# Layer norm sums moved from VectorE to ScalarE in a delta-rule attention kernel with two gated MLPs

## The chip, the cores and the metric

The kernel runs on one core of one Trainium2 chip. A core has TensorE (PE in the profile, with PEld for its weight loads), VectorE (DVE), ScalarE (ACT), GpSimd (POOL) and SyncE (SP), which here only issues DMAs. Each engine takes its instructions strictly in the order of its own list; between engines semaphores tell when something may start. The metric is the device time of one execution in microseconds (us), lower is better; a time of a kernel is the median of several runs.

## The reference

Three blocks follow one another, for batch 4, 8 heads, 768 positions, head size 48, so that the model width is 384:

```
state = 0                                   # delta-rule attention, per head
for t in range(S):
    y[t]  = q[t] @ state
    state = state + beta[t] * outer(kn[t], v[t] - kn[t] @ state)      # kn = k / |k|

gate = sigmoid(causal_conv5(y));  x = (gate * (y @ w_val)) @ w_out    # first MLP

h = gelu_tanh(x @ w_in)                     # second MLP; d_ff = 1024
u, v = h[:, :512], h[:, 512:]
v_n  = (v - mean(v)) / sqrt(var(v) + 1e-6) * g_ln                     # over the 512 features
v_s  = w_sg @ v_n + b_sg                    # mixes the 768 positions of a batch
out  = x + (u * v_s) @ w_out2
```

## The kernel before

**Attention.** The sequences are cut into chunks of 64 positions: 4 batches of 12 chunks, 48 steps (`seq(n)` and `attend(n)`), which follow one another, since each needs the state of the one before. Ahead of them the triangular systems of two chunks at a time are prepared (`norm`, `keys`, `gram`, `base`, `merge`); `base` solves for 8 chunks at once on VectorE, on tiles named X and tmp. Nearly every fp32 result is split into a high and a low fp16 half: ScalarE copies to the high half, then VectorE (or GpSimd) subtracts to get the low one, and TensorE multiplies halves in three passes (`mm3`). A step of the recurrence so goes back and forth between TensorE, ScalarE and VectorE (tiles rh, wh, mh, ys, qh, ps_q, ps_y, ps_state).

**MLPs.** Positions go in tiles of 256 (`TT`), 3 to a batch. `front` loads the attention's output and makes the gate, `value` the gated values (gvh), `hidden` the half v of the second MLP with its layer norm, `gates` the half u, `mix` the mixing of positions by w_sg (PE tile wg,vnh), `final` the output. `mix` of a batch needs the normed tiles (vnh) of all six position blocks of 128 in that batch, so all three calls of `hidden`.

**The layer norm in `hidden`.** There are 12 calls of `hidden`, each with two blocks (`NS` = 2) of 128 positions on the partitions and 512 features along the row, 24 blocks in all. For each block, ScalarE writes v = gelu(ps); VectorE takes BN_STATS of v (tile st) and BN_AGGR of st to mean and variance (tile mv). For both blocks together, VectorE then scales the variance and negates the mean (two small TENSOR_SCALAR, tile va), GpSimd raises the variance to the power -1/2 (rd) and multiplies the mean by it (mb). ScalarE norms in place, v = v * rd + mb, and copies to the high half of vnh, and GpSimd subtracts for the low half.

**Order.** A planner in the kernel (`Program`) records every operation with its tiles, takes the order of each engine from a table (`ORDER`, one list of numbers for each of the five engines), and runs through it with a cost for each operation (`cost`). Where it expects TensorE to wait over 0.3 us, it may put in a filler: a matmul that adds to an unused half of the bank ps_state (`filler`, operand minus). The fillers are in the program for good. All instructions are issued through one helper line, L108, so groups are told apart by tiles.

Of the kernel before, what the change touches and what calls it, by code (L numbers as in the profile page):

```python
# [39 lines left out]
class Program:  # L40
# [41 lines left out]
    def add(self, engine, method, call, kw):  # L82
# [3 lines left out]
        for k in ("out",) + self.READS:  # L86
            m = self.memory.get(kw[k].tensor.name) if isinstance(kw.get(k), bass.AP) else None
            if m:
                touched.append((m, k == "out", self.region(kw[k], m)))
# [123 lines left out]
class Pool:  # L213
# [5 lines left out]
    def tile(self, shape, dtype, name, tag=None, **kw):  # L219
# [233 lines left out]
def cost(op):  # L453
# [13 lines left out]
    if engine == "scalar":  # L467
        if apart:
            t = 0.00225 * n - (0.113 if psum else 0.07)
            return t, t + 0.26, False  # L470
# [925 lines left out]
```

## Time and profile before

| what | value |
|---|---|
| median of 3 runs | 647.62 us |
| lowest and highest of them | 646.28 and 649.8 us |
| the profiled execution, whole | 646.62 us |
| its span, first to last instruction | 644.7 us |
| granted TensorE clock, mean | 0.991 |

The profile is of one execution. Its own time is 1.92 us over its span, and 1.0 us under the median. A row of the profile gives an engine, an operation, the tiles it writes and reads, and its durations; idle time of an engine is listed by what ended it.

### The profile page before, as it was taken

Reading aid. Unit: us, or ns where it says so; the run is one execution under the profiler, and the core shown is the slowest. Engines: PE = TensorE matmul, PEld = TensorE weight load, DVE = VectorE, ACT = ScalarE, POOL = GpSimd, SP = SyncE. Lnnn points to the kernel's source line nnn. Section 1 sums busy time; section 2 is a strip of 40 time slices with the busy share of each in tenths; the row PEclk is TensorE's granted clock in tenths of the full one; section 3 lists DMA queues with packets and bytes.
Section 4 is the critical chain, followed back from the end, with each engine's and each line's share of the span. In section 5 each row is a group of like instructions: output and inputs, shape, how many; then the busy total and the mean of one; then the engine's idle time right before and its main releaser. Section 6 shows DMA issues by size and latency. Waiting matters only on the chain. (4 is left out here: it accounts for less than half of the span.)

```text
span 644.7 us, 23559 instructions
## 1 busy us (share of the span) xinstructions
PE 575.0 (89%) x9821; PEld 473.8 (73%) x9821; DVE 503.1 (78%) x1341; ACT 398.2 (62%) x932; POOL 179.6 (28%) x204
## 2 busy tenths in 40 slices
PE   0678879779979989799999999889999999999997
PEld 0555446668767767688888689778978897877886
DVE  7898998979889998988999879899887854562222
ACT  7886697756876767775466785344948544524221
POOL 7404041126423625366001650001605010303000
PEclk9999998989999998999999999999999999999999
DMA  7664367877579776687678778788687763211121
GB/s 223 160 202 132 126 189 235 186 156 165 107 182 175 134 122 146 128 195 132 163 143 179 145 123 170 121 140 152 120 155 141 107 142 102 63 50 34 58 82 50
DMA packets 288826, 89.22 MB, mean 138 GB/s; under 512 B 250704, under 2 KB 276944, under 8 KB 288720
## 3 DMA queue, kind: packets, MB, share of 16 engines
q1 hardware_dynamic: 288720, 87.72, 63.0%
q8 instruction: 77, 1.26, 0.9%
q14 instruction: 29, 0.24, 0.1%
HBM read 51.81 MB, written 23.33 MB: 117 GB/s over the span
## 5 line engine op out<-in xcount | busy, mean ns | idle before, releaser
L108 PE MATMUL ps_mlp<-wg,vnh 128*128 128x256 f16 x864 | 112.4, 272 | 1.4 <-DVE ps_mlp L108 1.4
L108 PEld LDWEIGHTS <-vnh 128*128 128x128 f16 x864 | 80.5, 97 | 12.0 <-issue 2.1
L108 PEld LDWEIGHTS <-kj 112*128 112x128 f16 (+1 forms) x1632 | 69.2, 97 | 21.4 <-issue 12.7
L108 PEld LDWEIGHTS <-kc 64*64 64x64 f16 x1920 | 42.1, 113 | 47.5 <-DVE kc L108 20.8
L108 PE MATMUL ps_mlp<-gvh,wi 128*128 128x256 f16 x432 | 58.0, 272 | 1.2 <-ACT v L108 0.8
L108 PE MATMUL ps_mlp<-gth,w 128*128 128x256 f16 x432 | 58.8, 272 | 0.0
L108 DVE TENSOR_TENSOR tmp<-X 128x84 f32<-128x84 f32 (+12 forms) x156 | 56.1, 360 | 1.4
L108 DVE TENSOR_TENSOR X<-X,tmp 128x84 f32<-128x84 f32 (+12 forms) x156 | 54.5, 349 | 1.5
L108 PE MATMUL ps_mlp<-wi,gvh 128*128 128x512 f16 x216 | 54.7, 379 | 0.6 <-ACT gvh L108 0.4
L108 DVE SCALAR_TENSOR_TENSOR ps_mlp<-ps_mlp,gl,bs 128x256 f32<-128x256 f32 x48 | 23.4, 488 | 34.3 <-PE ps_mlp L108 33.9
L108 DVE SCALAR_TENSOR_TENSOR a<-x,cw,a 128x256 f32<-128x256 f32 x108 | 48.8, 486 | 1.6 <-ACT a L108 1.3
L108 PE MATMUL ps_mlp<-xh,wv 128*128 128x256 f16 x324 | 45.7, 272 | 2.2 <-ACT xh L108 2.1
L108 PE MATMUL ps_mlp<-gvh,wo 128*128 128x256 f16 x324 | 47.1, 272 | 0.1
L108 PEld LDWEIGHTS <-m1p 128*128 128x128 f16 x1152 | 39.5, 96 | 9.9 <-issue 5.7
L108 PE MATMUL pk<-i,kc 64*64 64x64 f16 x704 | 22.5, 200 | 27.2 <-DVE kc L108 20.0
L108 PEld LDWEIGHTS <-wi 128*128 128x128 f16 x432 | 40.3, 97 | 6.4 <-issue 1.3
L108 PEld LDWEIGHTS <-w 128*128 128x128 f16 x432 | 40.8, 98 | 5.0
L108 PE MATMUL ps_y<-qh,kj 112*128 112x64 f16 x576 | 32.8, 193 | 4.2 <-ACT ys L108 4.1
L108 POOL TENSOR_TENSOR X<-X,bm 128x1024 f32<-128x1024 f32 x5 | 11.8, 2353 | 87.4 <-DVE X L108 72.0
L108 PEld LDWEIGHTS <-ws 128*128 128x128 f16 (+1 forms) x828 | 32.2, 98 | 4.9 <-issue 3.2
L108 PEld LDWEIGHTS <-wo 128*128 128x128 f16 x342 | 31.8, 97 | 5.5 <-issue 0.9
L108 POOL TENSOR_TENSOR vnh<-v,vnh 128x512 f16<-128x512 f32 x24 | 27.9, 1170 | 25.6 <-ACT vnh L108 25.5
(165 smaller groups left out, 1451.5 us busy)
## 6 DMA issues: line engine op xcount, KB each, us to landing
keys_d<-kc SPq DMA_DIRECT2D x22, 512.0 KB, 4.1
kj<-keys_d SPq DMA_DIRECT2D x44, 256.0 KB, 5.0
wg<-wgd SPq DMA_DIRECT2D x12, 768.0 KB, 4.8
ws<-wh SPq DMA_DIRECT2D x66, 96.0 KB, 3.6
qf<-in_qt SPq DMA_DIRECT2D x24, 224.0 KB, 3.5
kf<-in_kn SPq DMA_DIRECT2D x12, 384.0 KB, 4.7
vf<-in_vn SPq DMA_DIRECT2D x24, 192.0 KB, 3.4
xd<-ys SPq DMA_DIRECT2D x48, 96.0 KB, 3.0
```

What stands on the lines that cost most here:

```text
L108: op.call()
```

## The change

The statistics of the layer norm are no longer taken by VectorE. The Gelu pass on ScalarE writes, beside v, the sum of its 512 results to a tile `sums` (accum_out). GpSimd multiplies that sum by -1/512, which gives the negated mean (va). A new ScalarE pass then takes the square of v plus that negated mean, again with an accumulator, which gives the sum of the squared deviations; its 512 squares are written into the high half of vnh, which the later copy overwrites. GpSimd scales this sum to the variance. BN_STATS, BN_AGGR and the two TENSOR_SCALAR go; 24 Square passes on ScalarE and 36 small operations on GpSimd (24 of 128x1, 12 of 128x2) come. The planner learns that accum_out is written, and adds 0.093 to ScalarE's cost where there is one. All five lists of the order are made anew; the numbers in them say nothing to a reader, and one line stands for them.

```diff
-        for k in ("out",) + self.READS:
+        for k in ("out", "accum_out") + self.READS:
...
-                touched.append((m, k == "out", self.region(kw[k], m)))
+                touched.append((m, k in ("out", "accum_out"), self.region(kw[k], m)))
...
-        "3 14 18 6 13 16 0 12 15 5 22 19 24 11 20 25:2 10 47 17 4 7 1 8 35 2 21 23 32 38 9 37 36 34 33 28 30 29 31 "
+        "6 0 3 20:2 1 14 16 13 24 8 12 15 11 25:2 22 10 18 35 32 38 9 2 7 47 17 37 19 36 34 33 5 4 23 28 30 29 31 "
...
     if engine == "scalar":
+        more = 0.093 * ("accum_out" in op.kw)
...
-        return t, t + 0.1, False
+        return t + more, t + more + 0.1, False
...
-        mv = mp.tile([P, NS, 2], F32, name="mv", tag="mv", bufs=2)
+        sums = mp.tile([P, 2, NS], F32, name="sums", tag="mv", bufs=2)
+        va = mp.tile([P, 2, NS], F32, name="va", tag="va", bufs=2)
...
-            nc.scalar.activation(out=v, in_=ps, func=AF.Gelu_apprx_tanh, scale=1.0 / (SGV * SWI))
-            st = mp.tile([P, 6], F32, name="st", tag="st", bufs=2)
-            nc.vector.bn_stats(out=st, in_=v)
-            nc.vector.bn_aggr(out=mv[:, i], in_=st)
+            nc.scalar.activation(out=v, in_=ps, func=AF.Gelu_apprx_tanh, scale=1.0 / (SGV * SWI),
+                                 accum_out=sums[:, 0, i:i + 1])
+            nc.gpsimd.tensor_scalar(out=va[:, 1, i:i + 1], in0=sums[:, 0, i:i + 1], scalar1=-1.0 / HF, scalar2=None, op0=ALU.mult)
+            h = mp.tile([P, 2, HF], F16, name="vnh", tag="vnh", bufs=NVN)
+            nc.scalar.activation(out=h[:, 0], in_=v, func=AF.Square, bias=va[:, 1, i:i + 1], accum_out=sums[:, 1, i:i + 1])
+            kept["vn", b, tt * NS + i] = h
             vs.append(v)
-        va = mp.tile([P, 2, NS], F32, name="va", tag="va", bufs=2)
-        nc.vector.tensor_scalar(out=va[:, 0], in0=mv[:, :, 1], scalar1=SVN ** -2, scalar2=1e-6 * SVN ** -2, op0=ALU.mult,
+        nc.gpsimd.tensor_scalar(out=va[:, 0], in0=sums[:, 1], scalar1=SVN ** -2 / HF, scalar2=1e-6 * SVN ** -2, op0=ALU.mult,
                                 op1=ALU.add)
-        nc.vector.tensor_scalar(out=va[:, 1], in0=mv[:, :, 0], scalar1=-1.0, scalar2=None, op0=ALU.mult)
...
-            h = mp.tile([P, 2, HF], F16, name="vnh", tag="vnh", bufs=NVN)
+            h = kept["vn", b, tt * NS + i]
```

TensorE's list keeps its course: at the end of each of the 44 steps that update the state, the matmuls of the MLPs that stand ahead of it differ between the two lists by at most about ten. It holds 303 fillers now and held 268; of those between the 2,400th and the 3,300th other matmul, which is where the first two calls of `hidden` run, it holds 39 and held 11. The common operations of VectorE and ScalarE stand, on the mean, one place from where they stood.

VectorE, at the first call of `hidden` (batch 0, positions 0 to 255), before; X and tmp are the triangular solve, the rest but st, mv and va is the recurrence:

```order
L108 TENSOR_TENSOR mh<-ps_y,mh 128x256
L108 TENSOR_TENSOR X<-X,tmp 128x13x18
L108 SCALAR_TENSOR_TENSOR wh_109<-ps_state,wh_109 112x4x48
L108 TENSOR_TENSOR tmp<-X 128x238
L108 BN_AGGR mv<-st 128x2
L108 TENSOR_TENSOR X<-X,tmp 128x14x17
L108 BN_STATS st<-v 128x6
L108 TENSOR_TENSOR tmp<-X 128x240
L108 SCALAR_TENSOR_TENSOR tbd_94<-ps_b,tbd_94 32x8x32
L108 SCALAR_TENSOR_TENSOR rh<-ps_q,rh 128x192
L108 TENSOR_TENSOR X<-X,tmp 128x15x16
L108 BN_AGGR mv<-st 128x2
```

The same place of VectorE after the change:

```order
L108 TENSOR_TENSOR mh<-ps_y,mh 128x256
L108 TENSOR_TENSOR X<-X,tmp 128x13x18
L108 SCALAR_TENSOR_TENSOR wh_109<-ps_state,wh_109 112x4x48
L108 TENSOR_TENSOR tmp<-X 128x238
L108 SCALAR_TENSOR_TENSOR tbd_94<-ps_b,tbd_94 32x8x32
L108 TENSOR_TENSOR X<-X,tmp 128x14x17
L108 TENSOR_TENSOR tmp<-X 128x240
L108 SCALAR_TENSOR_TENSOR rh<-ps_q,rh 128x192
L108 TENSOR_TENSOR X<-X,tmp 128x15x16
```

The statistics are gone, and the recurrence's rows (tbd, rh) stand one row of the solve further up or down.

GpSimd, at the second call of `hidden` (batch 0, positions 256 to 511), before; tbh and tah are halves of the solved systems, xh of the attention's output:

```order
L108 TENSOR_TENSOR tbh<-tab,tbh 128x256
L108 TENSOR_TENSOR tbh<-tab,tbh 128x3x256
L108 TENSOR_TENSOR xh<-x,xh 128x780
L108 TENSOR_TENSOR tah<-tab,tah 128x256
L108 MEMSET x 128x3x4
L108 TENSOR_TENSOR tah<-tab,tah 128x3x256
L108 TENSOR_TENSOR qh<-qf,qh 112x256
L108 AFFINE_SELECT bm<-bt 128x1024
L108 TENSOR_TENSOR rd<-va,root 128x2
```

The same place of GpSimd after the change:

```order
L108 TENSOR_TENSOR tbh<-tab,tbh 128x256
L108 TENSOR_SCALAR va<-sums 128x1
L108 TENSOR_TENSOR tbh<-tab,tbh 128x3x256
L108 TENSOR_SCALAR va<-sums 128x1
L108 TENSOR_TENSOR xh<-x,xh 128x780
L108 MEMSET x 128x3x4
L108 TENSOR_TENSOR tah<-tab,tah 128x256
L108 TENSOR_SCALAR va<-sums 128x2
L108 TENSOR_TENSOR tah<-tab,tah 128x3x256
L108 TENSOR_TENSOR qh<-qf,qh 112x256
L108 AFFINE_SELECT bm<-bt 128x1024
L108 TENSOR_TENSOR rd<-va,root 128x2
```

Three small operations now stand between large ones, the second negation behind the larger subtraction for tbh; rd stays where it was.

ScalarE, at the last call of `hidden` (batch 3, positions 512 to 767), before:

```order
L108 ACTIVATE v<-ps_mlp 128x512 x2
L108 ACTIVATE bs<-bs 128x256
L108 ACTIVATE u<-ps_mlp 128x512
L108 ACTIVATE v<-v,mb,rd 128x512 x2
L108 ACTIVATE vnh<-v 128x512
```

The same place of ScalarE after the change:

```order
L108 ACTIVATE v,sums<-ps_mlp 128x512 x2
L108 ACTIVATE vnh,sums<-v,va 128x512 x2
L108 ACTIVATE u<-ps_mlp 128x512
L108 ACTIVATE v<-v,mb,rd 128x512
L108 ACTIVATE vnh<-v 128x512
```

The two Squares (vnh,sums) stand directly behind the two Gelus, and the norm of the second block behind the copy of the first.

## Rows read from the trace of the kernel before

**Rows 1.** The page: span, then busy time and its share by engine.

```profile
span 644.7 us, 23559 instructions
PE 575.0 (89%) x9821; PEld 473.8 (73%) x9821; DVE 503.1 (78%) x1341; ACT 398.2 (62%) x932; POOL 179.6 (28%) x204
```

**Rows 2.** Busy time of each engine in three stretches; the first row names the columns.

```profile
core 0: us, PE busy (x) PEld busy (x) DVE busy (x) ACT busy (x) POOL busy (x), PEclk, DMA share, GB/s
...
160.00:290.00 130.00, 116.86 (x2532) 97.21 (x2531) 116.42 (x326) 94.42 (x225) 56.26 (x60) 0.99 0.74 148
290.00:548.00 258.00, 250.30 (x4234) 214.91 (x4232) 213.74 (x568) 154.11 (x367) 58.25 (x57) 1.00 0.75 140
548.00:640.00 92.00, 91.15 (x811) 77.50 (x809) 35.17 (x78) 28.91 (x53) 11.31 (x13) 1.00 0.17 55
```

**Rows 3.** PE's waits from 290 to 548 us: sum in us, times, longest.

```profile
PE ps_b L108 <- DMA m1p<-gx: 2.7, 2, 1.4
PE ps_y L108 <- DMA ws<-wh: 1.9, 3, 1.4
PE ps_y L108 <- ACT ys L108: 1.4, 2, 0.7
PE ps_y L108 <- ACT rh L108: 0.5, 1, 0.5
```

**Rows 4.** Busy DVE time of BN_STATS and BN_AGGR (tile st) in two stretches of rows 2.

```profile
160.00:290.00 130.00, 4.82 (x12) 0.99 0.74 148
290.00:548.00 258.00, 11.16 (x26) 1.00 0.75 140
```

**Rows 5.** Groups by shape: busy us, mean ns of one | idle before.

```profile
L108 DVE BATCH_NORM_STATS2 st<-v 128x6 f32<-128x512 f32 x24 | 16.1, 685 | 6.9 <-ACT v L108 6.8
...
L108 DVE BATCH_NORM_AGGREGATE mv<-st 128x2 f32<-128x6 f32 x24 | 3.8, 171 | 0.0
...
L108 DVE TENSOR_SCALAR va<-mv 128x2 f32<-128x2 f32 x24 | 3.7, 185 | 0.4
```

**Rows 6.** Groups by shape: ScalarE's passes over 128x512 from SBUF, with and without per-partition operands.

```profile
L108 ACT ACTIVATE v<-v,mb,rd 128x512 f32<-128x512 f32 x24 | 18.8, 805 | 1.3 <-POOL mb L108 1.1
...
L108 ACT ACTIVATE vnh<-v 128x512 f16<-128x512 f32 x24 | 14.8, 623 | 0.1
```

**Rows 7.** GpSimd's small operations: ns min/median/max, first and last start.

```profile
L108 POOL TENSOR_TENSOR rd<-va,root x12: 688/702/853, 184.3 to 586.9; 128x2 f32<-128x2 f32 x12
L108 POOL TENSOR_TENSOR mb<-va,rd x12: 190/195/451, 185.8 to 587.7; 128x2 f32<-128x2 f32 x12
```

**Rows 8.** PE, PEld and POOL time with the filler's operand (minus), from 160 to 290 us.

```profile
160.00:290.00 130.00, 5.99 (x49) 3.50 (x49) 0.00 (x0) 0.99 0.74 148
```

**Rows 9.** Timeline around the last call of `hidden`: start, us, what, idle before it.

```profile
584.44 1.11 ACT L108 ACTIVATE v<-ps_mlp 128x512 f32<-128x512 f32 x2 [0.23 <-PE ps_mlp L108]
...
586.93 0.69 POOL L108 TENSOR_TENSOR rd<-va,root 128x2 f32<-128x2 f32 x1 [0.89 <-DVE va L108]
...
587.73 2.56 PE L108 MATMUL ps_mlp<-wg,vnh 128*128 128x256 f16 x22
...
592.36 0.33 PEld L108 LDWEIGHTS <-vnh 128*128 128x128 f16 x4 [0.24 <-POOL vnh L108]
```

**Rows 10.** GpSimd's timeline at the second call of `hidden`.

```profile
211.51 2.31 POOL L108 TENSOR_TENSOR tbh<-tab,tbh 128x768 f16<-128x768 f32 x1 [0.81 <-ACT tbh L108]
```

**Rows 11.** DVE's longest wait from 160 to 290 us.

```profile
DVE wh L108 <- ACT wh L108: 2.7, 5, 0.7
```

**Rows 12.** ScalarE's Square and Gelu (min/median/max, first and last start), and its table loads.

```profile
L108 ACT ACTIVATE sq<-kf x24: 505/515/572, 4.0 to 281.2; 128x384 f32<-128x384 f32 x24
...
L108 ACT ACTIVATE v<-ps_mlp x24: 591/597/617, 176.8 to 585.0; 128x512 f32<-128x512 f32 x24
...
L108 ACT ACT_TABLE_LOAD x2 | 2.6, 1283 | 0.8 <-PEq L1383 0.8
```

More of the change, by code (lines that the diff above doesn't have):

```diff
@@ L1212, in hidden @@
             nc.scalar.activation(out=v, in_=v, func=AF.Identity, scale=rd[:, i:i + 1], bias=mb[:, i:i + 1])
-            h = mp.tile([P, 2, HF], F16, name="vnh", tag="vnh", bufs=NVN)
+            h = kept["vn", b, tt * NS + i]
             nc.scalar.activation(out=h[:, 0], in_=v, func=AF.Copy)
             nc.gpsimd.tensor_tensor(out=h[:, 1], in0=v, in1=h[:, 0], op=ALU.subtract)
-            kept["vn", b, tt * NS + i] = h
     def gates(b, tt):
```

392 rows, old and new, of tables (gpsimd, scalar, sync, tensor) are left out of this document.

## The prediction

> **What bounds the kernel now.** I read the page's busy shares first, then the busy time by stretches, then who waits for whom. The shares alone mislead: TensorE is busy 89% of the span and VectorE 78% [rows 1], which looks like a kernel bound by TensorE throughout. The stretches [rows 2] tell it apart. From 290 to 548 us TensorE is busy 250.3 of 258 us, from 548 to 640 us 91.2 of 92 us. There its own matmuls set the time, and all that any other engine can give back is its 7.7 + 0.9 us of idle time. From 160 to 290 us it is busy 116.9 of 130 us, of which 6.0 us have to do with fillers [rows 8], so it does without some 19 us. In that stretch VectorE is busy 116.4 us, 90%, with the triangular solve and the recurrence mixed in one list, and ScalarE 94.4 us, 73%. The first Gelu of `hidden` starts at 176.8 us [rows 12], so what the change replaces lies behind that.
>
> So the statistics lie in three places: 6 of the 24 blocks in the stretch from 160 to 290 us, which I call A; 13 in B, 290 to 548 us; and the other 5 in the tail, where TensorE alone works through the MLPs (two operations to a block [rows 4]).
>
> **What goes.** The three groups of VectorE are busy 16.1 + 3.8 + 3.7 = 23.6 us [rows 5], 0.98 us a block. That is 5.9 us in A, 12.8 us in B, 4.9 us in the tail.
>
> **What comes on ScalarE.** A Square over 128x512 from SBUF with one per-partition operand (the negated mean as bias). The trace has such a pass with no such operand, 0.623 us, and with two, 0.805 us [rows 6]; I take the middle, 0.714 us, which says 0.091 us for an operand. An accumulator is not in the trace. Two are written for each block, one by the Gelu, one by the Square. From below each could cost nothing; from above I take a small operation of its own, 0.195 us as GpSimd's mb [rows 7]. A gain is excluded, since the pass itself does not get shorter. I choose 0.091 us, what an operand with one value a partition costs on that engine. So a block adds 0.714 + 0.182 = 0.90 us to ScalarE, with ends of 0.62 and 1.20 us: 5.4 us in A (3.7 to 7.2), 11.7 us in B.
>
> **What comes on GpSimd.** 36 operations on one or two values a partition. Of that size the trace has mb, 0.195 us, and rd, 0.70 us, which is a power [rows 7]; a multiplication is nearer to mb. That makes 7.0 us on an engine that is busy 28% [rows 1]; hidden as time, but the first 24 stand between a Gelu and the Square that follows it, and the Square stands in ScalarE's list ahead of parts of the recurrence (mh, rh, wh). This is the one wait that the change adds. Where a large subtraction runs on GpSimd, such as the 2.31 us of tbh at the second call [rows 10], the negation behind it waits, and with it the Square and all of ScalarE's list.
>
> **A.** VectorE is 90% busy; I count its relief at that share, 5.9 x 0.90 = 5.3 us. ScalarE is 73% busy; what it gets I count at that share, 5.4 x 0.73 = 3.9 us. VectorE's longest wait there is for ScalarE, the high half of wh [rows 11], so the two engines take turns on one path and the one price is set against the other: **-1.4 us**.
>
> **The fillers.** 35 more are issued, whatever TensorE then has to do. Where it waits anyhow they cost nothing; where it doesn't, a matmul of 256 columns takes up to 2.56 / 22 = 0.12 us [rows 9], 4.1 us together at most. They stand mostly in A, where TensorE has 13 us of idle time [rows 2]: **+0.5 us**. They are no measure of a wait, but they stand where the planner expects one.
>
> **B.** VectorE gives 12.8 us at 83% and ScalarE takes 11.7 us at 60%, a net 3.6 us of relief; but it can act only through TensorE's 7.7 us of idle time. Of the waits listed, 1.9 us are for ScalarE and 4.6 us for DMAs that carry the recurrence's tiles [rows 3]. I take **-0.8 us**.
>
> **The tail.** TensorE waits 0.24 us for the last vnh [rows 9], so its cover is used up at that place and the chain's length counts. Before: the last Gelu ends at 584.44 + 1.11 = 585.55 us, rd begins at 586.93 us: 1.38 us. After: two Squares, 2 x 0.80 us with accumulator, stand directly behind the Gelus; the first's negation is done under the second Gelu, the second's under the first Square; then the variance, 0.195 us, and the hand-overs, some 0.1 us; with the Gelu's own accumulator 1.98 us. That is **+0.6 us** (0 to 1.2).
>
> **The sum** against the profiled execution, 646.62 us: -1.4 + 0.5 - 0.8 + 0.6 = -1.1, so 645.5 us. The median of the runs lies 1.0 us above that execution, so **646.5 us** is forecast. A measurement of this kernel can tell about 0.5%, 3.2 us, from no change; the forecast is within it.
>
> **Rivals.**
> *VectorE alone is the bound.* Then ScalarE's additions fit into its 35.6 us of idle time in A, the 5.9 us come off whole, and in B half of the DMAs' 4.6 us goes with the earlier recurrence and 1.9 us of the waits for ScalarE too, 4.2 us; fillers and tail cost nothing. 647.6 - 10.1 = 637.5 us. For it: 90% in A; against it: VectorE itself waits there for ScalarE.
> *ScalarE and GpSimd take the place of VectorE: slower.* The place is A, the Square behind its negation. Each of 6 Squares holds ScalarE's list for 1.0 us (half of the subtraction of 2.31 us, less what lies under the Gelu), and the recurrence behind it: +6 us there, and 1 us more in B; 646.5 + 7 = 653.5 us. It decides from 1.4 / 6 = 0.23 us a Square on, from where A loses. For it: the order puts the negations between large subtractions, and 39 fillers where 11 were. Against it: in the first call of `hidden` GpSimd has nothing large to do, and in the tail neither.
> *The tables.* A Square between Gelus could need another set of function tables and so two loads for each block. One load takes 1.283 us, but there are two in the whole trace, while Squares run up to 281 us and Gelus from 177 us on [rows 12]; so both stand in one set here. With two loads for each of 24 blocks it would be 24 x 2 x 1.283 = 61.6 us on ScalarE, and 708 us at worst.
> The Trainium skill, "ScalarE: Activation LUTs", section "Table sets: the hidden batching unit", has the rule that speaks against a pass of squares between Gelus: functions are loaded in sets, and calls are to be batched by set. By that page's estimate of 2.66 us a switch the sum would be 646.5 + 24 x 2 x 2.66 = 774 us. The trace does not agree that it applies here: two loads.
>
> **Chances.** Forecast 0.57; VectorE alone 0.20; slower 0.22; tables 0.01. About the forecast I allow 3.5 us to each side (accumulator's ends 1.3 us in A, fillers 3.6, tail 0.6, median of three runs 1), so a fifth of it, 0.12, falls under 644.4 us, and 0.02 over 650.9 us. Faster by over 0.5%: 0.20 + 0.12 = 0.32. Slower: 0.22 + 0.01 + 0.02 = 0.25. Within: 0.43. The range leaves out half of each rival: 638 to 653.5 us.
>
> **What would show it.** Right: VectorE's busy time falls by about 23 us, ScalarE's grows by about 21 us, and TensorE's busy time from 290 us on stays at 97% or more. The Square's mean duration tells the accumulator's price (0.80 us forecast; 0.71 free, 0.91 dear). ScalarE waiting for va on GpSimd for more than 1.4 us in A, or rh and wh late behind a Square, speaks for the slower rival; the last `ys` before 290 us earlier by 5 us or more, with ScalarE's idle time shrunk, for VectorE alone. More than two table loads would overthrow the third. I am wrong if the order, made anew, shifts the recurrence in A by more than the 5 us of work that change places; the trace of before cannot show that.

## The result: slower by 1.15%

The changed kernel takes 654.03 us (median of 20 runs, 647.19 to 657.22), the kernel before, run beside it on the same chip, 645.67 us (20 runs, 641.38 to 650.02). The ratio is 1.0115, 95% interval 1.0092 to 1.0137; it is worked out from the single runs and so differs a little from the quotient of the two medians (1.0129). Here and below the ratios leave out a kernel's markedly slow runs. The profiled execution spans 653.8 us, against 644.7 before.

The head of the page after, which answers to [rows 1]:

```profile
span 653.8 us, 23651 instructions
...
PE 583.6 (89%) x9856; PEld 479.8 (73%) x9856; DVE 483.0 (74%) x1269; ACT 417.0 (64%) x1004; POOL 189.1 (29%) x240
```

VectorE's busy time fell by 20.1 us, ScalarE's grew by 18.8 us, GpSimd's by 9.5 us. The exchange happened as the diff says, at nearly equal amounts, and the time went up by 7 to 8 us. The same three stretches as in [rows 2], after the change:

```profile
160.00:290.00 130.00, 115.34 (x2344) 93.78 (x2341) 104.69 (x289) 90.98 (x227) 52.29 (x65) 0.95 0.69 133
290.00:548.00 258.00, 250.64 (x4351) 216.19 (x4347) 206.61 (x535) 167.00 (x410) 68.74 (x79) 1.00 0.78 143
548.00:640.00 92.00, 90.47 (x811) 75.68 (x810) 32.28 (x65) 36.71 (x77) 13.31 (x22) 1.00 0.19 61
```

In the first stretch everybody is less busy than before, VectorE by 11.7 us, ScalarE by 3.4 us although it got more to do: the work of the stretch moved to later. The granted clock is 0.95 there against 0.99. What TensorE waited for in that stretch, before and then after (engine, tile, who came last: sum in us, times, longest):

```profile
PE ps_y L108 <- ACT ys L108: 2.1, 4, 0.9
PE ps_state L108 <- ACT wh L108: 1.3, 3, 0.4
```

```profile
PE ps_state L108 <- ACT wh L108: 3.5, 5, 1.9
PE ps_y L108 <- ACT ys L108: 3.0, 3, 1.2
```

Both are tiles of the recurrence that ScalarE writes; ScalarE delivers them later.

The new operations in groups by shape (busy us, mean ns of one | idle before), to be read beside [rows 5 to 7]:

```profile
L108 ACT ACTIVATE vnh<-v,va 128x512 f16<-128x512 f32 x24 | 17.2, 718 | 1.3 <-POOL va L108 1.0
...
L108 POOL TENSOR_SCALAR va<-sums 128x1 f32<-128x1 f32 x24 | 6.2, 258 | 90.5 <-ACT v L108 90.3
...
L108 ACT ACTIVATION_READ_ACCUMULATOR v<-ps_mlp 128x1 f32 x24 | 4.8, 198 | 0.0
...
L108 ACT ACTIVATION_READ_ACCUMULATOR vnh<-v,va 128x1 f32 x24 | 4.6, 193 | 0.0
...
L108 ACT ACT_TABLE_LOAD x2 | 2.6, 1283 | 0.8 <-PEq L1380 0.8
...
L108 POOL TENSOR_SCALAR va<-sums 128x2 f32<-128x2 f32 x12 | 2.4, 196 | 8.8 <-ACT vnh L108 8.3
```

The Square takes 0.718 us. An accumulator is an instruction of its own, a read of one value a partition. The first row's last part says that the Squares waited for GpSimd's negation (va) for 1.0 us in the whole run.

**A clock made of the recurrence.** ScalarE copies one result tile `ys` for each of 48 steps, so its starts tell how far the recurrence is. The table gives the start in the kernel before, and how much later the same step starts in another kernel's profiled execution, with the difference at the step at 171 us, ahead of the first call of `hidden`, set to zero. It is worked out from the starts in the traces; it compares single executions, which differ by -3.1 to +3.6 us at 171 us already, so it shows where a loss arises and not how large it is.

```
step at (us, before)                 183    217    249    284    379    494    553
after                               +2.2   +5.3   +7.2   +9.5  +10.2   +9.9  +10.8
e1  the change, order of before     +1.8   +2.3   +4.2   +3.8   +6.9   +9.7  +10.5
e3  Squares added                   +1.8   +3.6   +4.8   +4.7   +7.0   +8.7   +9.1
e4  no statistics                   +1.0   +2.4   +2.6   +1.8   +0.6   +0.8   +1.0
e5  Squares added, late             +0.1   +0.6   +0.9   +1.3   +2.9   +3.5   +3.2
e10 as e3, more fillers             +1.6   +2.6   +3.5   +3.0   +9.7   +8.3   +8.2
e11 as e4, more fillers             +1.6   +0.6   +0.6   -0.5   +4.7   +3.9   +3.3
e12 the change, Squares late        +0.1   +2.7   +2.0   +2.1   +3.1   +3.3   +3.8
e13 Squares in first three calls    +1.8   +2.5   +3.9   +3.8   +3.1   +3.8   +4.3
e14 Squares in the other nine calls  0.0   +1.1   +1.5   +0.9   +3.5   +5.9   +6.9
```

(e14's profiled execution took 657.3 us, the longest of its 12, whose median is 651.51, so its row is to be read with care.) In the changed kernel nearly all of the loss arises between 171 and 284 us, in stretch A. The same operations in the order of before (e1) lose as much in all, but 3.8 us of it by 284 us and 6.7 us behind.

### The profile page after: what moved, and what is told of

The parts are those of the page before. It is cut to its first block, busy times and chain, and to the rows that moved or that the text cites. A ratio compares the mean times of both kernels' runs of the same rounds, so it can differ in the third digit from the quotient of the medians.

```text
span 653.8 us, 23651 instructions
## 1 busy us (share of the span) xinstructions
PE 583.6 (89%) x9856; PEld 479.8 (73%) x9856; DVE 483.0 (74%) x1269; ACT 417.0 (64%) x1004; POOL 189.1 (29%) x240
## 4 chain that ended last, share of the span: by engine, by line
PE 56%; DVE 14%; ACT 13%; DMA 9%; issue 4%; POOL 2%; SPq 0%; ACTq 0%; DVEq 0%; POOLq 0%
PE ps_mlp L108 39%; PE ps_y L108 6%; PE ps_q L108 4%; PE pk L108 4%; DVE X L108 3%; PE ps_state L108 3%; PE ps_b L108 2%; DMA wst<-in_w_in 2%; DVE tmp L108 2%; ACT v L108 1%; DMA m1p<-gx 1%; DMA xd<-ys 1%; ACT vnh L108 1%; ACT kc L108 1%; DMA x<-xd 1%
## 5 line engine op out<-in xcount | busy, mean ns | idle before, releaser
L108 PEld LDWEIGHTS <-kc 64*64 64x64 f16 x1920 | 43.6, 114 | 45.7 <-DVE kc L108 20.7
L108 PE MATMUL ps_state<-minus 128*128 128x256 f16 (+1 forms) x303 | 36.0, 282 | 3.0 <-ACT wh L108 2.9
L108 PEld LDWEIGHTS <-ws 128*128 128x128 f16 (+1 forms) x828 | 33.9, 98 | 4.9 <-issue 2.6
L108 POOL TENSOR_SCALAR va<-sums 128x1 f32<-128x1 f32 (+1 forms) x36 | 8.5, 237 | 99.2 <-ACT v L108 90.3
```

Of the source, the lines that this page charges most:

```text
L108: op.call()
```

## Experiments

All ratios are against the kernel before, run beside it on the same chip. In every kernel but e2 (and the change itself) the order of the lists and the 268 fillers are those of before, written out as fixed tables, so that only the named edit differs: an operation that is added, left out or moved, or the 59 more fillers of e10 and e11.

### The change taken apart: order, ScalarE's part, VectorE's part

**e1**, the change's operations in before's order; **e2**, the reverse.

```diff
 (e1: the changed kernel)
-ORDER, fillers: drawn for the change
+ORDER, fillers: those of before
 (e2: the kernel before)
-ORDER, fillers: those of before
+ORDER, fillers: drawn for the change
```

> The changed kernel's operations (sums by ScalarE, Squares, GpSimd's small ones) in the order of the kernel before: all that the two kernels share stands on each engine as before, the 24 Squares and 36 small operations stand behind the same neighbour as in the changed kernel, and the 268 fillers are at their places of before. Theory O, the order made anew costs the time: ratio to before 1.000, 643 to 647 us. Theory S, the passes and accumulator reads on ScalarE cost it: 1.010 or more, 652 us or more.

> The kernel before's operations (BN_STATS and BN_AGGR on VectorE) in the order and with the 303 fillers of the changed kernel; VectorE's statistics stand behind the same neighbour as before. Theory O: 1.010 or more, 652 us or more. Theory S: 0.997 to 1.003, about 645 us.

Measured: e1 657.07 us, 1.0163 (1.0127 to 1.0199); e2 667.13 us, 1.0313 (1.0273 to 1.0354). So the new order is not what costs the new operations their time: in the old order the kernel with them is, if anything, slower than the change (1.0115; the intervals overlap). But the old operations in the new order are the slowest of all, so in the new order the same exchange of operations gains about 2%, where in the old one it costs 1.6%. Each order serves the operations that it was drawn for, and a price found in one does not hold in the other. The runs below take the exchange apart in before's order; what its parts are worth in the new order was not tried.

**e3** puts ScalarE's part alone onto the kernel before, which keeps its statistics; **e4** takes VectorE's statistics out and puts nothing in their place.

```diff
 (e3)
-            nc.scalar.activation(out=v, in_=ps, func=AF.Gelu_apprx_tanh, scale=1.0 / (SGV * SWI))
...
+            nc.scalar.activation(out=v, in_=ps, func=AF.Gelu_apprx_tanh, scale=1.0 / (SGV * SWI), accum_out=st[:, 6:7])
...
+            nc.scalar.activation(out=h[:, 0], in_=v, func=AF.Square, bias=zero, accum_out=st[:, 7:8])
```

```diff
 (e4)
-            nc.vector.bn_stats(out=st, in_=v)
-            nc.vector.bn_aggr(out=mv[:, i], in_=st)
...
```

> The kernel before with ScalarE's part of the change added and nothing taken away: the Gelu writes its sum, a Square pass with an accumulator follows for each block (24 of them, bias from a column of zeros, so that it waits for no other engine), the statistics stay on VectorE; order and fillers of before. ScalarE gets about 19 us more. Theory S: 1.010 or more, 652 us or more. Theory O: 0.998 to 1.005.

> The kernel before without BN_STATS and BN_AGGR, 20 us of VectorE's busy time (left out: the variance is a constant and the mean an element of v, so the output is another); the two small TENSOR_SCALAR of a call stay; order and fillers of before. It gives the worth of VectorE's relief alone. By the prediction's steps A gains about 4 us and B about 2, 639 to 642 us (0.993); if VectorE alone bounds A, 635 to 638 us (0.985); if its relief lands in waits, 644 to 646 us (1.000).

Measured: e3 655.80 us, 1.0124 (1.0081 to 1.0167); e4 645.63 us, 0.9992 (0.9959 to 1.0024). In before's order ScalarE's part alone gives a loss as large as the change's, about 8.0 us. VectorE's relief, 14.4 us less busy time (488.7 against 503.1 us), is worth nothing that can be measured; by the interval it gains 0.4% at most. Two of VectorE's waits from 160 to 290 us in e4 tell where it went:

```profile
DVE wh L108 <- ACT wh L108: 6.3, 6, 3.1
DVE ps_y L108 <- PE ps_y L108: 4.7, 5, 1.7
```

The first was 2.7 us before [rows 11], the second 2.1:

```profile
DVE ps_y L108 <- PE ps_y L108: 2.1, 3, 1.0
```

The relief turned into waits for ScalarE and TensorE. One place in detail, VectorE's mask on ps_y at the first call of `hidden`, in the timeline of before and then of e4 (start, us, what, idle before it):

```profile
178.90 0.43 DVE L108 SCALAR_TENSOR_TENSOR ps_y<-ps_y,cmask 128x256 f32<-128x256 f32 x1 [0.46 <-PE ps_y L108]
```

```profile
178.19 0.43 DVE L108 SCALAR_TENSOR_TENSOR ps_y<-ps_y,cmask 128x256 f32<-128x256 f32 x1 [1.72 <-PE ps_y L108]
```

Where a BN_STATS and a row of the solve had stood ahead of it, VectorE now waits 1.3 us longer for the same matmul. (e4's mask is 0.71 us earlier, and e4 is 0.7 us earlier at 171 us already.)

### Place or amount: why ScalarE's part costs

The second call of `hidden` in ScalarE's timeline before:

```profile
211.80 0.39 ACT L108 ACTIVATE ys<-ps_y 112x256 f32<-112x256 f32 x1
212.06 0.62 ACT L108 ACTIVATE v<-ps_mlp 128x512 f32<-128x512 f32 x1
212.54 0.44 ACT L108 ACTIVATE qf<-qf 112x256 f32<-112x256 f32 x1
212.94 0.33 ACT L108 ACTIVATE rh<-ps_q 128x192 f16<-128x192 f32 x1
213.32 0.39 ACT L108 ACTIVATE mh<-ps_y 128x256 f16<-128x256 f32 x1
213.77 0.85 ACT L108 ACTIVATE xh<-x 128x780 f16<-128x780 f32 x1
214.65 0.38 ACT L108 ACTIVATE m1p<-ps_b 32x256 f16<-32x256 f32 x1
215.06 0.33 ACT L108 ACTIVATE wh<-ps_q 128x192 f16<-128x192 f32 x1
...
216.08 0.65 ACT L108 ACTIVATE tah<-tab 128x256 f16<-128x256 f32 x1 [0.38 <-DVE tab L108]
216.64 0.36 ACT L108 ACTIVATE ys<-ps_y 112x256 f32<-112x256 f32 x1
```

And in e3, which is 1.25 us later when it comes there:

```profile
213.05 0.40 ACT L108 ACTIVATE ys<-ps_y 112x256 f32<-112x256 f32 x1
213.32 0.75 ACT L108 ACTIVATE vnh<-v,zero 128x512 f16<-128x512 f32 x1
213.93 0.22 ACT L108 ACTIVATION_READ_ACCUMULATOR vnh<-v,zero 128x1 f32 x1
214.03 0.62 ACT L108 ACTIVATE v<-ps_mlp 128x512 f32<-128x512 f32 x1
214.50 0.23 ACT L108 ACTIVATION_READ_ACCUMULATOR v<-ps_mlp 128x1 f32 x1
214.59 0.44 ACT L108 ACTIVATE qf<-qf 112x256 f32<-112x256 f32 x1
214.90 0.36 ACT L108 ACTIVATE rh<-ps_q 128x192 f16<-128x192 f32 x1
215.11 0.42 ACT L108 ACTIVATE mh<-ps_y 128x256 f16<-128x256 f32 x1
216.36 0.85 ACT L108 ACTIVATE xh<-x 128x780 f16<-128x780 f32 x1 [0.82 <-DMA x<-xd]
217.12 0.71 ACT L108 ACTIVATE vnh<-v,zero 128x512 f16<-128x512 f32 x1
...
217.94 0.38 ACT L108 ACTIVATE m1p<-ps_b 32x256 f16<-32x256 f32 x1
218.34 0.33 ACT L108 ACTIVATE wh<-ps_q 128x192 f16<-128x192 f32 x1
```

No row of e3 ahead of xh has idle time in brackets: ScalarE goes from one to the next without a pause. rh and mh, which the recurrence waits for, start 2.0 and 1.8 us later than before, so 0.7 and 0.5 us of their delay arose here, behind a Square and two reads. xh starts 2.6 us later, 1.3 us of it here, with a wait for its own tile on top. The second Square stands between xh and wh, which starts 3.3 us later, 2.0 us of it here; TensorE waits 0.5 us for it at 218.7 us, and the next `ys` is 2.6 us further behind than the one at 211.8 us (+1.0 us there and +3.6 us at the next, counted as in the table). In **e5** each Square alone is moved to where before's trace shows ScalarE idle.

```diff
-ORDER scalar: ... Gelu, ys, Square, Gelu, qf, rh, mh, xh, Square ...
+ORDER scalar: ... Gelu, ys, Gelu, qf, rh, mh, xh, m1p, wh, qf, Square, tah, ys ...
```

> The kernel before, statistics and all, with the 24 Squares and the 48 accumulators of e3 added, but each Square stands in ScalarE's list where the trace of before shows ScalarE idle, between the Gelu and the norm of the same block (19 of the 24 in front of an instruction that waited over 0.25 us there). The sums of ScalarE are not used. Theory 'place' (a Square costs because it stands ahead of instructions of the recurrence that are ready): most of e3's 1.2% goes, ratio 0.999 to 1.004, about 646 to 649 us. Theory 'amount' (ScalarE's list has no room, 0.9 us more in it is 0.3 to 0.4 us later wherever it stands): ratio 1.010 to 1.014, about 652.5 to 655 us.

Measured: 648.50 us, 1.0052 (1.0020 to 1.0085). "Amount" falls (the two names are those of the theories above), and "place" holds for the larger part: 0.72 of the 1.24% is gone with the same instructions in another place. The value lies a little above the span that "place" gave, so some of the price stays. The same place in e5's timeline:

```profile
213.94 0.71 ACT L108 ACTIVATE vnh<-v,zero 128x512 f16<-128x512 f32 x1
214.55 0.19 ACT L108 ACTIVATION_READ_ACCUMULATOR vnh<-v,zero 128x1 f32 x1
214.64 0.64 ACT L108 ACTIVATE tah<-tab 128x256 f16<-128x256 f32 x1
215.54 0.38 ACT L108 ACTIVATE ys<-ps_y 112x256 f32<-112x256 f32 x1 [0.26 <-PE ps_y L108]
```

The Square fills the 0.38 us in which ScalarE waited for VectorE's tab, and ScalarE still arrives at ys before TensorE has it.

**e6** leaves the accumulators out of e3.

```diff
-..., func=AF.Square, bias=zero, accum_out=st[:, 7:8])
+..., func=AF.Square, bias=zero)
```

> e3 without its accumulators: the 24 Squares as bare passes at the same places, the Gelus as before; the Squares' results are not used. If the passes carry the price by their busy time (24 x 0.714 of some 18.8 us), ratio about 1.011, 653 us. If the 48 reads of the accumulator, 0.19 us each, carry it because each stops ScalarE between two instructions (24 x 2 x 0.19 = 9.1 us against 17.1 us of passes), ratio about 1.008 or less, 651 us or less.

Measured: 652.29 us, 1.0092 (1.0053 to 1.0130). The passes carry most of it; that the reads carry the other 0.3% can't be told, the intervals of e3 and e6 overlap.

**e12** is the whole change in before's order with the Squares late.

```diff
-ORDER scalar, gpsimd: as e1
+ORDER scalar, gpsimd: each Square at an idle place of ScalarE, GpSimd's sums behind it
```

> The whole change in before's order, as e1, but each Square where before's trace shows ScalarE idle or nearly so, 1.9 us or more ahead of the norm where there is such a place. Theory 'place': it gives back what e5 gave back against e3 (0.7%), so ratio 1.006 to 1.011, about 650 to 653 us, and with VectorE relieved no more than that. Theory 'amount': as e1, 1.014 to 1.018, about 655 to 657.5 us. Third: the norm now waits for the late Square, its variance and the power on GpSimd, and the MLP behind it: 1.015 or more, with ScalarE waiting over 5 us in all for mb.

Measured: 651.70 us, 1.0085 (1.0056 to 1.0113), against e1's 1.0163 (1.0127 to 1.0199). "Place" again, in the full change: 0.78%, about 5 us, comes back, and still the kernel doesn't reach the one before. The third theory, a norm that waits over 5 us for mb, did not come: ScalarE waits 2.0 us for mb in all of e12.

### Relief in the other direction

If ScalarE's list is on the path, taking a pass off it should gain. **e7** gives the copy to the high half to VectorE, **e8** the norm too; **e9** leaves the copy out.

```diff
 (e7)
-            nc.scalar.activation(out=h[:, 0], in_=v, func=AF.Copy)
+            nc.vector.tensor_copy(out=h[:, 0], in_=v)
 (e8, and e7's)
-            nc.scalar.activation(out=v, in_=v, func=AF.Identity, scale=rd[:, i:i + 1], bias=mb[:, i:i + 1])
+            nc.vector.tensor_scalar(out=v, in0=v, scalar1=rd[:, i:i + 1], scalar2=mb[:, i:i + 1], op0=ALU.mult, op1=ALU.add)
 (e9)
-            nc.scalar.activation(out=v, in_=v, func=AF.Identity, scale=rd[:, i:i + 1], bias=mb[:, i:i + 1])
-            nc.scalar.activation(out=h[:, 0], in_=v, func=AF.Copy)
+            nc.scalar.activation(out=h[:, 0], in_=v, func=AF.Identity, scale=rd[:, i:i + 1], bias=mb[:, i:i + 1])
```

> The kernel before, with one of ScalarE's passes of each block given to VectorE: the copy of the normed block to its high half (vnh<-v, 24 x 0.623 = 15.0 us), put in VectorE's list where that copy started on ScalarE. Theory S (ScalarE's list is on the path and VectorE's is not): the reverse of e3, at its price of 8.0 us for 18.8 us of busy time, so -6.4 us, ratio 0.990, about 640 us. Rival (what e3 cost was the hold-up at the places of its Squares, and ScalarE's list as a whole has slack): ratio 0.997 to 1.003. If VectorE's list is as much on the path, its part eats the relief: 1.000 or above.

> As e7, and the norm itself (v<-v,mb,rd, 24 x 0.805 = 19.3 us) on VectorE too: 34.3 us off ScalarE. Theory S: -34.3 x 0.43 = -14.6 us, ratio 0.977, about 631 us, less what TensorE's own matmuls from 290 us on don't let through (some 4 us of that), so 0.98 to 0.985. Rival 'place': 0.997 to 1.003. If VectorE's list is as much on the path: 1.000 or above, and more than e7.

> The kernel before, with 24 of ScalarE's passes left out and nothing put in their place: the norm writes the high half itself, and the copy to it (24 x 0.623 = 15.0 us) is gone; GpSimd subtracts it from the block that was not normed, so the low halves are not the reference's. The counterpart of e4 for ScalarE. If a microsecond off ScalarE is worth what one on it costs in e3 (8.0 us for 18.8): -6.4 us, ratio 0.990, about 639.5 us. If relief of one engine alone finds the next wait at once, as e4 found for VectorE: 0.997 to 1.002. The second makes e7's 1.0075 the price of VectorE's side alone.

Measured: e7 651.24 us, 1.0075 (1.0042 to 1.0108); e8 656.83 us, 1.0139 (1.0091 to 1.0188); e9 646.92 us, 1.0006 (0.9972 to 1.0040). The theory that ScalarE's list as a whole is on the path, and VectorE's is not, falls here. 13 us less busy time on ScalarE (e9, 385.1 against 398.2 us) are worth as little as the statistics off VectorE, and the same copy put onto VectorE, 0.57 us each and waiting for ScalarE's norm, costs 0.75%:

```profile
L108 DVE CAST vnh<-v 128x512 f16<-128x512 f32 x24 | 13.6, 570 | 3.2 <-ACT v L108 3.1
```

In before's order neither engine's busy time as such sets the time: relief of one ends in the next wait, for another engine or for a DMA. In e9, for instance, TensorE waits for these from 160 to 290 us, where before it waits for neither:

```profile
PE ps_y L108 <- DMA ws<-wh: 1.5, 1, 1.5
...
PE ps_mlp L108 <- DMA ws<-wh: 1.2, 1, 1.2
```

On ScalarE e3 against e5 shows that an added pass costs by what stands behind it. That the copies on VectorE cost by the same mechanism is likely but not shown: they also wait 3.1 us for ScalarE's norm, and no run moved them.

### The clock of TensorE

In e3's trace the granted clock is 0.5, the lower of the two levels (1.2 GHz), for 6.8 us at 180.2 us and for 3.4 us each at 217.8 and 251.9; in before's only for 3.4 us at 247.4 in that stretch, after the change four times 3.4 us. TensorE had waited ahead of each. But e4, whose median loses nothing, has as much of it there as e3: 10.2 us at 178.9 and 3.4 us at 216.5. Are the low stretches the loss? **e10** and **e11** put 59 fillers into those waits, onto e3 and onto e4.

```diff
 FILLS = {
...
+    7091: 16, 7072: 16, ... 6340: 10, 6311: 5, ... 5820: 12, ...
```

> e3 with 59 more filler matmuls of TensorE, put into the five waits ahead of which its trace shows the granted clock at 0.5 (at 177, 179, 212, 214 and 246 us of before's trace). Theory 'clock' (what e3 costs is made of the stretches at 0.5: 6.8 us at 180.2, 3.4 at 217.8, 3.4 at 251.9, against one of 3.4 before): they go, and with them half of e3's 1.2% or more, ratio 1.000 to 1.007, 646 to 650.5 us. Theory 'list' (instructions of the recurrence behind the Squares are late whatever the clock): 1.010 to 1.015, 652.5 to 656 us.

> e4 (statistics left out: the variance is a constant and the mean an element of v, so the norm is not the reference's) with the same 59 fillers. Its trace shows the clock at 0.5 for 10.2 us at 178.9 and 3.4 us at 216.5. If the relief of VectorE was there and the clock ate it: ratio 0.993 to 0.997, 641.5 to 644 us. If VectorE's relief is worth nothing: 0.998 to 1.003.

Measured: e10 656.32 us, 1.0152 (1.0096 to 1.0207); e11 649.52 us, 1.0040 (1.0010 to 1.0069). The low stretches up to 285 us did go, the row of that stretch in e10 shows the clock at 1.00:

```profile
160.00:290.00 130.00, 115.58 (x2517) 96.22 (x2516) 114.09 (x315) 96.83 (x238) 55.46 (x59) 1.00 0.72 146
```

and still the time didn't fall. But the fillers brought a cost of their own: both kernels have a stop of TensorE of 2.1 us, which ends at 289.9 us in e10 and at 288.1 us in e11 (below), and 3.4 us at clock 0.5 from 289.5 and 289.3 us, and the next `ys`, at 296 us of before, is 3.7 and 3.9 us further behind than the one at 284.

```profile
PE ps_mlp L108 <- issue: 2.1, 1, 2.1
```

So "clock" does not hold as the main cause: up to 284 us, with the clock at 1.00, e10 still loses 3.0 us. That the low clock adds to it (e3 lost 4.7 us by there, and e4 went from +1.8 to e11's -0.5) is what single traces suggest; the runs don't separate it from the new stop.

### Where it arises

**e13** and **e14** split e3 by calls of `hidden`.

```diff
 (e13)
+            more = dict(accum_out=st[:, 6:7]) if b == 0 else {}
...
+            if b == 0:
                 nc.scalar.activation(out=h[:, 0], in_=v, func=AF.Square, bias=zero, accum_out=st[:, 7:8])
 (e14)
+            more = dict(accum_out=st[:, 6:7]) if b else {}
...
+            if b:
                 nc.scalar.activation(out=h[:, 0], in_=v, func=AF.Square, bias=zero, accum_out=st[:, 7:8])
```

> e3 with its Squares and accumulators in the first three calls of hidden alone (6 of 24 blocks, the stretch A). If what ScalarE gets costs time only where TensorE has idle time to hide behind, as the prediction has it (A -1.4, B -0.8 us), nearly all of e3's 1.24% is here: ratio 1.010 or more, 652.5 us. If it costs by its place in every call, as e3's own ys say (4.7 of 9.1 us by 284 us): 1.005 to 1.008, 649 to 651 us.

> The rest of e3: Squares and accumulators in the nine calls behind 290 us (18 of 24 blocks; B and the tail). If TensorE's own matmuls set the time there and have 7.7 us of idle time at most: 0.998 to 1.003. If the place counts there too: 1.004 to 1.007, 648.5 to 650.5 us.

Measured: e13 651.68 us, 1.0066 (1.0038 to 1.0094); e14 651.51 us, 1.0077 (1.0046 to 1.0108). The two parts add up to e3 within the intervals (0.66 + 0.77 = 1.43 against 1.24%). Six blocks in A cost as much as eighteen behind it, but the eighteen are not free, as they should have been if TensorE's own matmuls alone set the time there.

## Why the prediction was wrong

The forecast was 646.5 us, within 0.5% of before; measured is 654.0 us, slower, half a microsecond above the range. (In its chances a fifth of 0.57 is 0.11 and not 0.12; nothing hangs on it.) By its steps:

- **The amounts were right.** Square 0.714 us forecast, 0.718 measured. The accumulator's 0.091 us is right for the slot, though not for the instruction: a read lasts 0.19 to 0.20 us but starts some 0.1 us before the end of the pass ahead and lets the next start some 0.1 us after its own start (in e3: pass 213.32, read 213.93, next pass 214.03). VectorE -20 us for 23 forecast and ScalarE +19 for 21: operations overlap by about 0.1 us, so sums of durations say too much. TensorE is busy 341.1 of 350 us from 290 us on, 97.5%, as forecast.
- **A, -1.4 us, is the step that failed, and in it VectorE's relief.** I counted VectorE's relief at VectorE's busy share (0.90), 5.3 us, and ScalarE's additions at ScalarE's (0.73), 3.9 us, as if work on an engine were on the path with that probability. In before's order e4 says 0 for the relief of all 24 blocks, where by the same reckoning A alone was to give some 4 us (e4 keeps the two small TENSOR_SCALAR); e13 says +0.66%, 4.3 us, for ScalarE's additions in A alone. So the additions came out near their term, and the relief that was to outweigh them was not there. That the additions fit the busy share is luck: e5 adds the same work in other places at 0.42 of e3's price. What tells is the place: whether an instruction stands ahead of something that is ready, or fills a wait.
- **The rest of A's loss is open.** The changed kernel is 9.5 us behind by 284 us and e1, the same operations in before's order, 3.8 us; the 5.7 us between these two single traces are about the sign that the prediction named for being wrong, a shift of the recurrence in A by the order of more than 5 us. The new order makes it up behind 284 us, where e1 loses 6.7 us and the change 1.3. How much of it is the order and how much the clock, which is low four times in A, the runs don't separate.
- **B, -0.8 us: near, by luck.** By the table the changed kernel loses 1.3 us behind 284 us. But e1 and e3 lose 6.7 and 4.4 us there: TensorE's 7.7 us of idle time bounds what can be won there, not what can be lost, and e14 loses 5.0 us in B and the tail.
- **The tail, +0.6 us, was right for the chain, but does not show in the time.** From the last Gelu's end (593.51 + 0.59 = 594.10 us) to rd at 596.07 us it is 1.97 us, against 1.98 forecast, and TensorE's matmuls now wait 0.8 us for the last vnh, where before only the weight load did, 0.24 us [rows 9]:

```profile
593.51 0.59 ACT L108 ACTIVATE v<-ps_mlp 128x512 f32<-128x512 f32 x1
```

```profile
596.07 0.72 POOL L108 TENSOR_TENSOR rd<-va,root 128x2 f32<-128x2 f32 x1
```

```profile
PE ps_mlp L108 <- POOL vnh L108: 0.8, 1, 0.8
```

  From the last `ys` to the end of the span, though, the changed kernel takes 91.2 us and the one before 91.7, each in one execution.
- **The fillers, +0.5 us,** were not measured by themselves. In A the operations on the fillers' operand take 11.5 us of TensorE for 6.0 before [rows 8], 78 of them for 49; e1, with the fillers of before, is no faster than the change. The 59 others cost some 3 us in e11 against e4 (the intervals just overlap) and nothing that can be told apart in e10 against e3; the stop of 2.1 us that came with them may be the reason.
- **The slower rival** had the sign, the stretch and nearly the time (653.5 us), by another mechanism. Of its two signs one came: rh and wh late behind a Square, in e3. But it had the Square hold up ScalarE's list while it waits for GpSimd's negation, 1.0 us each. Of that the trace shows 1.0 us in all; even in e1 it is 3.9 us:

```profile
ACT vnh L108 <- POOL va L108: 1.0, 2, 0.7
```

```profile
ACT vnh L108 <- POOL va L108: 3.9, 8, 0.9
```

  The Square needs no wait to do harm: e3, whose Squares wait for no negation, loses as much. There the Square is ready, and its own 0.7 us is what stands ahead of rh, mh, xh and wh.
- **VectorE alone is the bound:** refuted by e4, in before's order. **The tables:** two loads after as before; more than two would have spoken for this rival. The Trainium skill's rule on batching by table set ("ScalarE: Activation LUTs", section "Table sets: the hidden batching unit") doesn't reach this change; Square and Gelu share what is loaded here.

What stays open: why the change keeps 0.85% with its Squares late (e12), about half of what it loses in before's order (e1), of which GpSimd's sums, the reads behind the Gelus and the places that I chose each may be part; the share of the clock; and what ScalarE's part and VectorE's relief are worth in the new order, in which the changed kernel itself runs.

## What to carry to other kernels

In a kernel whose lists are interleaved by hand or by a planner, an engine's busy share says neither what relief is worth nor what an addition costs. Look at the instruction behind the edited place: if it waits anyhow, removing work gains little (e4 and e9 nothing measurable) and adding work costs little (e5 0.52%); if it is ready and another engine waits for it, much of the added duration can go through (0.7 us to rh in the place that was read, and 1.24% in all of e3). Price both directions apart, by leaving the one part out and by adding the other alone, before the parts are set off against each other, and do not carry a price from one order to another.

## What the runs showed of the hardware

- Accumulating on ScalarE is an instruction of its own, ACTIVATION_READ_ACCUMULATOR, 0.193 to 0.198 us for 128x1, of which some 0.08 us is additional time on the engine in the place shown (from the start of a Gelu to the next pass 0.48 us before, at 212.06, and 0.56 us in e3, at 214.03).
- On VectorE a copy of 128x512 from f32 to f16 takes 0.570 us in e7 and 0.447 us in e8, where it follows the norm on the same engine; on ScalarE it takes 0.623 us [rows 6].
- TensorE stopped for up to 2.1 us with nothing that the profile shows to wait for. With the added fillers e10 and e11 have such a stop at the same matmuls, where e3 and e4 have none; what causes it was not tried.
